# Layer 2's down projection in a seven-product form over six pairs of inner tiles, in a two-layer FNet + GLU kernel

## The chip, the cores and the metric

One core of one Trainium2 chip runs the whole program in one launch. The metric is device time in microseconds (us). TensorE (PE) multiplies, VectorE (DVE), ScalarE (ACT) and GpSimd (POOL) do the elementwise work, and transfers are started from SyncE's queue (SP) and from GpSimd's queue. PSUM has eight banks, each of 512 fp32 numbers in 128 partitions.

## The reference

`x` is 2048 tokens by 640. Two layers, each a Fourier mixing and a gated linear unit (GLU), both with a residual:

```python
def _A_ref(x, dft_seq_re, dft_seq_im, dft_hid_re, dft_hid_im):
    a = jnp.einsum("bsd,ed->bse", x, dft_hid_re)
    b = jnp.einsum("bsd,ed->bse", x, dft_hid_im)
    return jnp.einsum("ts,bse->bte", dft_seq_re, a) - jnp.einsum("ts,bse->bte", dft_seq_im, b)

def _B_ref(x, w_gate, w_up, w_down):          # 640 x 1728, 640 x 1728, 1728 x 640
    g = jnp.einsum("bsd,df->bsf", x, w_gate)
    u = jnp.einsum("bsd,df->bsf", x, w_up)
    return jnp.einsum("bsf,fd->bsd", _sigmoid(g) * u, w_down)

for _ in range(2):
    x = x + _A_ref(_layernorm(x), dft_seq_re, dft_seq_im, dft_hid_re, dft_hid_im)
    x = x + _B_ref(_layernorm(x), w_gate, w_up, w_down)
```

All is fp32. The same weights serve both layers.

## The kernel before

**Numbers.** A value is kept as two fp16 parts, HI and LO, and a product is three matmuls (`PASSES`: HI x HI, HI x LO, LO x HI) added up in PSUM. To make parts, ScalarE copies a value to fp16 (HI), and VectorE subtracts that copy from it (LO).

**Tiling.** The tokens are four blocks (`NB`) of 512, each four token tiles of 128. The inner size 1728 is 13 tiles of 128 (0 to 12) and a tail tile (13) of 64, which takes two passes. The output's 640 columns are two halves of 320 (`EH`). X (all tokens, fp32) stays on the chip. The rest lives in slots of one large buffer, `big`, which an allocator (`Slots`) gives out in units while the program is built.

**Order.** Nothing is scheduled by a planner: the order is written out by hand. `steps` is a list of steps, each with its matmuls (`mm`) and what follows them (`post`); `at(u, f, ...)` puts a job (a load, a split, a test) at a fractional time u in steps, and the jobs between two steps are issued there. An engine's instructions run in the order of issue, and so do the transfers of a queue.

**A layer's mixing** uses the symmetries of the Fourier matrices. As the matrices are inputs, the program reads them and tests these symmetries as it runs: GpSimd's queue loads pieces (L1293, L1310, L1353) into two rooms, VectorE compares them (L1299 to L1302), ScalarE squares and sums the differences (L1277). If a test fails, a general path runs in place of this one. For layer 2 the loads of these tests are spread evenly from 8 steps into block 0's gate-up to the end of block 2's.

**A layer's GLU**, block by block: gate and up for the block, then the down.
- Block 0's gate-up (`gate_up`, L1051): per inner tile 30 matmuls of 512 columns, each tile a step of its own; the tiles' PSUM banks come from a pool of eight, oldest first (`bank`, `free_bank`). Beside block 0 run the last combinations of the mixing for later tokens (`combine`, `join_hidden`, `add_hidden`, L920 to L940), in layer 2 partly beside block 1.
- Blocks 1 to 3 (`seven`, L1097): gate and up in a form with seven products. Two inner tiles share a step of 108 matmuls of 256 columns, in this order, with the counts of a step: `part_one` 12, `part_two` 18, `part_four` of an earlier tile 9, `part_six` 12 (the first that reads S), `part_four` 9, `part_five` 12, `part_seven` 18, `part_three` 18. Snaps (L1101) copy a PSUM chain to SBUF. `gate`, `up` and `up_parts` of the two tiles of the step before are issued between them: the sigmoid, the multiplications (L1153, L1155) after the sums (L1133, L1134), the parts of h (L1164, L1165). The last step has tile 12 and the tail (L1180, L1227 to L1231).
- Weights come back from DRAM for each block: `load_s` loads G (320 KB), S (512 KB, L1024) and U (192 KB) of one tile on SP's queue, about two steps ahead of the tile.
- The down (`down`, L1244): per token tile 41 products x 2 halves, 328 matmuls of 320 columns for a block; the evictions (L1259) add PSUM to X, and in layer 2 `store_x` stores the result right behind (L382 to L386 on SP's queue, and an indirect store, L378, on GpSimd's for two token tiles).

The down's loop before:

```python
order = [(j, hp, wp, e) for j in range(j0, j1) for hp, wps in (PASSES if j < NF else PASSES[:1])
         for wp in wps for e in es]
for j, hp, wp, e in order:
    nc.tensor.matmul(held["pd", e][0][:, :EH], held["ht", j].parts[hp][:, i * P : (i + 1) * P],
                     held["w", 2, j].parts[wp][:, e * EH : (e + 1) * EH], ...)
```

## Time and profile before

| | |
|---|---|
| median of 3 runs | 1162.23 us (1160.39 to 1162.62) |
| the profiled execution | 1158.61 us |
| its span | 1156.8 us |
| granted TensorE clock, mean | 0.999 |
| TensorE busy | 1127.3 us, 97%, 8784 matmuls |
| VectorE busy | 738.5 us, 64% |
| ScalarE busy | 507.7 us, 44% |
| GpSimd busy | 368.4 us, 32% |
| layer 2's GLU in the profile | 649.2 to 1150.4 us |

In a row of the chain the columns are the start, the length, the engine, what it is and its count. In a row of the windows: the stretch, its length, then busy time and count of PE, PEld (weight loads), DVE, ACT, POOL, then the granted clock, the DMA engines' busy share and GB/s. In a row of the groups: line, engine, operation, output<-input with shapes, count | busy us, mean ns of one | idle time of the engine just before them and what ended it. In a row of the timeline: start, length, engine, line, and in brackets the idle time before and its releaser.

### The profile page before, as it was taken

To read this page: it belongs to the slowest core of one execution; us is meant where nothing else is said; L and a number is where in the kernel's file an instruction comes from. 1 tells how busy PE (TensorE), PEld (TensorE's weight loads), DVE (VectorE), ACT (ScalarE), POOL (GpSimd) and SP (SyncE) were. 2 spreads that over 40 slices of the span, in tenths; PEclk is the share of its full clock that TensorE was granted. 3 is DMA by queue.
4 is the path that set the end of the run, shared out by engine and by line. 5 is a ranking of instruction groups with operands and counts; after the bars stand their busy time and mean duration, and the time that the engine had idled before them with its cause. 6 is when DMAs were issued, how large, how long until landed. Compare 5 with 4: busy or idle time off the path is not lost.

```text
span 1156.8 us, 22767 instructions
## 1 busy us (share of the span) xinstructions
PE 1127.3 (97%) x8784; PEld 860.0 (74%) x8784; DVE 738.5 (64%) x1636; ACT 507.7 (44%) x1094; POOL 368.4 (32%) x581
## 2 busy tenths in 40 slices
...
GB/s 267 148 46 236 241 355 281 259 209 212 144 265 182 252 179 194 264 191 258 47 18 110 190 200 73 129 264 262 222 142 258 247 270 56 199 240 184 132 19 38
DMA packets 158693, 216.46 MB, mean 187 GB/s; under 512 B 70194, under 2 KB 103883, under 8 KB 158574
## 3 DMA queue, kind: packets, MB, share of 16 engines
...
## 4 chain that ended last, share of the span: by engine, by line
PE 84%; DMA 2%; ACT 1%; POOL 1%; DVE 0%; issue 0%; SPq 0%; DVEq 0%; POOLq 0%
PE acc L1097 40%; PE acc L1244 31%; PE acc L1051 8%; PE acc L855 2%; PE acc L1180 2%; PE acc L773 1%; DMA kept_s<-big 1%; DMA kept_w<-big 1%; ACT big L236 1%; DVE big L238 0%; POOL big L1001 0%; PE acc L523 0%; ACT big L479 0%; ACT big L480 0%; POOL big L999 0%
## 5 line engine op out<-in xcount | busy, mean ns | idle before, releaser
L1097 PE MATMUL acc<-big 128*128 128x256 f16 x4212 | 462.8, 273 | 0.0
L1097 PEld LDWEIGHTS <-big 128*128 128x128 f16 x4212 | 412.1, 98 | 48.2
L1244 PE MATMUL acc<-big 128*128 128x320 f16 x2624 | 357.7, 299 | 0.0
L1244 PEld LDWEIGHTS <-big 128*128 128x128 f16 x2624 | 256.7, 98 | 99.7
L1293 POOL DMA_DIRECT2D big<-in_ct x256 | 175.1, 689 | 232.5 <-DVE big L1302 108.0
L1101 ACT ACTIVATE big<-acc 128x256 f32<-128x256 f32 x312 | 116.1, 381 | 208.9 <-PE acc L1097 207.5
L1051 PE MATMUL acc<-big 128*128 128x512 f16 (+1 forms) x990 | 176.5, 340 | 0.8 <-ACT big L236 0.5
L1051 PEld LDWEIGHTS <-big 128*128 128x128 f16 x990 | 96.5, 98 | 79.8 <-ACT big L236 1.0
L1277 ACT ACTIVATE big<-big 128x768 f32<-128x768 f32 (+8 forms) x104 | 79.4, 764 | 112.5 <-DVE big L1302 80.4
L1165 DVE TENSOR_TENSOR big<-big 128x512 f16<-128x512 f32 x78 | 53.8, 689 | 108.9 <-ACT big L1164 108.9
L1259 DVE SCALAR_TENSOR_TENSOR big<-acc,big 128x320 f32<-128x320 f32 x64 | 28.4, 484 | 91.6 <-PE acc L1244 91.5
L238 DVE SCALAR_TENSOR_TENSOR big<-big 128x640 f16<-128x640 f32 (+6 forms) x81 | 64.4, 833 | 2.9 <-ACT big L236 2.3
L1143 ACT ACTIVATE big<-big 128x512 f32<-128x512 f32 x78 | 47.9, 627 | 41.4 <-DVE big L1134 41.2
L236 ACT ACTIVATE big<-big 128x640 f16<-128x640 f32 (+7 forms) x81 | 50.7, 665 | 16.6 <-POOL big L1001 5.3
L1310 POOL DMA_DIRECT2D big<-in_ct x40 | 27.3, 686 | 94.9 <-ACT big L1277 47.3
L1134 DVE TENSOR_TENSOR big<-big,acc 128x512 f32<-128x512 f32 x78 | 53.1, 681 | 3.3 <-PE acc L1097 3.1
L1164 ACT ACTIVATE big<-big 128x512 f16<-128x512 f32 x78 | 48.8, 626 | 7.1 <-DVE big L1155 6.3
L1153 DVE SCALAR_TENSOR_TENSOR big<-acc,big 128x256 f32<-128x256 f32 x78 | 32.6, 418 | 27.9 <-PE acc L1097 22.4
L1299 DVE TENSOR_TENSOR big<-big 128x256 f32<-128x256 f32 x64 | 26.6, 416 | 36.8 <-DMA big<-in_ct 36.8
L855 PE MATMUL acc<-big 128*128 128x321 f16 (+3 forms) x324 | 48.8, 300 | 1.0 <-DVE big L238 1.0
L1300 DVE TENSOR_TENSOR big<-big 128x256 f32<-128x256 f32 x64 | 26.9, 421 | 30.9 <-DMA big<-in_ct 30.9
L509 ACT ACTIVATE big<-big 128x384 f16<-128x384 f32 (+2 forms) x48 | 28.9, 647 | 37.6 <-DVE big L491 17.9
...
## 6 DMA issues: line engine op xcount, KB each, us to landing
...
big<-in_ct POOLq DMA_DIRECT2D x256, 128.0 KB, 4.7
...
big<-in_ct POOLq DMA_DIRECT2D x32, 256.0 KB, 3.9
...
```

The costliest lines, as they stand in the source:

```text
L236: nc.scalar.activation(dh, src, AF.Copy, scale=s)
L238: nc.vector.scalar_tensor_tensor(dl, src, s, dh, op0=OP.mult, op1=OP.subtract)
L855: nc.tensor.matmul(ps[:m, :EC], z[:, at : at + m], w[:, 384 * wp : 384 * wp + EC], start=(d == 0 and zp == HI and wp == HI), stop=(d == ND ...
L1051: nc.tensor.matmul(ps, w[wp][:, d * P : (d + 1) * P], xt[:, xp, :], start=(d == 0 and wp == HI and xp == HI), stop=(d == ND - 1 and wp == LO))
L1097: nc.tensor.matmul(ps, wt, xt, start=start and n == 0, stop=n == len(todo) - 1, skip_group_check=not start)
L1101: nc.scalar.activation(dst, ps, AF.Copy)
L1134: nc.vector.tensor_tensor(v, v, other, op=OP.add)
L1164: nc.scalar.activation(s.parts[HI], v, AF.Copy)
L1165: nc.vector.tensor_tensor(s.parts[LO], v, s.parts[HI], op=OP.subtract)
L1244: nc.tensor.matmul(held["pd", e][0][:, :EH], held["ht", j].parts[hp][:, i * P : (i + 1) * P], held["w", 2, j].parts[wp][:, e * EH : (e + 1 ...
L1277: nc.scalar.activation(v, v, AF.Square, accum_out=new_sum()[:p])
L1293: nc.gpsimd.dma_start(v[:, g], bass.AP(ct.tensor, (r * S + row) * S, [[P, NS], [d * S, 16], [1, P]]))
```

## The change

In layer 2 the downs of all four blocks are written in a seven-product form. Inner tiles 0 to 11 make six pairs (`NP`). For a pair, h is a 2 x 2 matrix of parts (two halves of 256 tokens by two inner tiles) and the down weights another (two inner tiles by two halves of 320 columns). Seven products replace eight; four sums of h (A, AS) and four sums of weights (T1 to T4) are formed in exchange. The seven products go into four PSUM chains for each token tile (`CHAIN`), and a chain is added to X after every product (`READ`), which is 16 evictions for a block. Tiles 12 and 13 stay as they were (`REST`). The down's matmuls are 7 x 2 x 6 x 3 = 252 and 40, in place of 328.

With it go:
- `first_parts`, `second_parts`, `sum_parts` form and split the sums of h in the gate-up stages, in place of `gated_parts` and `up_parts`' two operations;
- T1 to T4 are formed from the raw weights in layer 1's downs of blocks 1 and 2 (`load_raw`, `make_t`, `split_t`, `keep_t`) and kept in DRAM. T1 comes with the down weights; T2, T3 and T4 (983 KB each) are loaded in each block of layer 2 on GpSimd's queue (`load_t`). `load_others` and `test_others` load and test the halves of weights that no longer come whole;
- stores of blocks 0 to 2 are issued in the next block's gate-up (`store_later`);
- layer 2's tests are spread anew: 11 in block 0's gate-up, 16 and 15 around blocks 1 and 2, and a test follows its load by 1.4 paces in place of one;
- all of layer 2's combines and joins lie in block 0's gate-up;
- for tiles from 4 on, `load_s` is split: S about one step ahead of its use, U at the step (before: all two steps ahead); for tiles 0 to 3 the loads move later in the down before;
- the allocator gets fixed places for A and AS and a limit for the others, G and U of a tile share one slot, and a row is written to DRAM and read again in layer 1;
- the scales `DS` and `PH` change by powers of two.

The core of the diff:

```diff
-DS = 2.0**11
+DS = 2.0**9
...
+NP = 6
+PAIRED = (), (0, 1, 2, 3)
...
+    def store_later(b, g, c):
+        if b < NB - 1:
+            at(block[b + 1] + 2.2 + 1.2 * g + c.start / D, store_x, b, g, c)
+        else:
+            store_x(b, g, c)
...
-    def load_s(j):
-        nc.sync.dma_start(take(5, "G", j).f16, kept["w", 0, j])
-        if ("S", j) not in held:
+    def load_s(j, do="GSU"):
+        if "G" in do:
+            v = take(8, "GU", j).f32
+            held["G", j], held["U", j] = Slot(v[:, : 5 * UNIT], None), Slot(v[:, 5 * UNIT :], None)
+            nc.sync.dma_start(held["G", j].f16, kept["w", 0, j])
+        if "S" in do and ("S", j) not in held:
             nc.sync.dma_start(take(8, "S", j).f16, kept["s", j])
-        nc.sync.dma_start(take(3, "U", j).f16.rearrange("p (q c) -> p q c", q=2),
-                          kept["w", 1, j].rearrange("p (q c) -> p q c", q=2)[:, :, 256:])
+        if "U" in do:
+            nc.sync.dma_start(held["U", j].f16.rearrange("p (q c) -> p q c", q=2),
+                              kept["w", 1, j].rearrange("p (q c) -> p q c", q=2)[:, :, 256:])
...
-    def gated_parts(j):
+    def gated_parts(j, paired=False):
+        if paired and j < 2 * NP:
+            if j % 2 == 0:
+                first_parts(j // 2, held["hf", j].f32)
+            else:
+                second_parts(j // 2, held["hf", j - 1].f32, held["hf", j].f32)
+                sum_parts(j // 2)
+                for i in (j - 1, j):
+                    drop("hf", i)
+            return
...
+    def up_parts(j, paired):
         if j not in late:
             return
         late.remove(j)
+        if paired and j < 2 * NP:
+            if j % 2 == 0:
+                first_parts(j // 2, held["hv", j].f32)
+            else:
+                second_parts(j // 2, held["hv", j - 1].f32, held["hv", j].f32)
+                for i in (j - 1, j):
+                    drop("hv", i)
+            return
...
+            if paired and j > 0:
+                sum_parts(j // 2 - 1)
...
+    def first_parts(p, v):
+        a = both(take(6, "A", p, top=UNITS - 8 * NP), 768)[:, :, :256]
+        f = take(8, "af", p).f32
+        nc.vector.tensor_tensor(f[:, 512:768], v[:, :256], v[:, 256:], op=OP.subtract)
+        nc.scalar.activation(a[:, 0], v[:, :256], AF.Copy)
+        nc.vector.tensor_tensor(a[:, 1], v[:, :256], a[:, 0], op=OP.subtract)
+    def second_parts(p, v, w):
+        a, f = both(held["A", p], 768)[:, :, 256:], held["af", p].f32
+        s1, s2, s4 = (f[:, 256 * n : 256 * (n + 1)] for n in (0, 1, 3))
+        nc.scalar.activation(a[:, 0], w, AF.Copy)
+        nc.vector.tensor_tensor(s1, v[:, 256:], w[:, 256:], op=OP.add)
+        nc.vector.tensor_tensor(s2, s1, v[:, :256], op=OP.subtract)
+        nc.vector.tensor_tensor(s4, w[:, :256], s2, op=OP.subtract)
+        nc.vector.tensor_tensor(a[:, 1], w, a[:, 0], op=OP.subtract)
+    def sum_parts(p):
+        f, s = held["af", p].f32, both(take(8, "AS", p, top=UNITS), 1024)
+        for c in (slice(0, 512), slice(512, 1024)):
+            nc.scalar.activation(s[:, 0, c], f[:, c], AF.Copy)
+        for c in (slice(0, 512), slice(512, 1024)):
+            nc.vector.tensor_tensor(s[:, 1, c], f[:, c], s[:, 0, c], op=OP.subtract)
+        drop("af", p)
...
+    def make_t(p):
+        v, w = (held["dr", 2 * p + k].f32 for k in range(2))
+        b11, b12, b21, b22 = v[:, :EH], v[:, EH:], w[:, :EH], w[:, EH:]
+        nc.vector.tensor_tensor(b11, b12, b11, op=OP.subtract)
+        nc.vector.tensor_tensor(b12, b22, b12, op=OP.subtract)
+        nc.vector.tensor_tensor(b22, b22, b11, op=OP.subtract)
+        nc.vector.tensor_tensor(b21, b21, b22, op=OP.subtract)
...
+    def load_t(n, b, p=None):
+        if n == 1:
+            nc.sync.dma_start(take_t(n, b, p), kept["t", n][:, p])
+            return
+        take_t(n, b, 0)
+        v = held["T4"].f16 if n == 4 else t_place(n, b)
+        nc.gpsimd.dma_start(v.rearrange("p (k q c) -> p k q c", k=NP, q=2), kept["t", n])
...
+    LEFT = {1: ("A", 0), 2: ("A", 1), 4: ("A", 2), 5: ("AS", 0), 6: ("AS", 1), 7: ("AS", 2), 3: ("AS", 3)}
+    RIGHT = {1: (0, 0), 2: (1, 0), 3: (1, 1)}
+    CHAIN = {1: "a", 2: "c", 5: "b", 3: "b", 4: "d", 6: "a", 7: "a", 8: "a"}
+    READ = {1: (0, 0), 2: (0, 0), 5: (1, 1), 3: (0, 1), 4: (1, 0), 6: (0, 1), 7: (1, 0), 8: (1, 1)}
+    REST = (2, 3, 4, 8)
...
+            for n, i in todo:
+                first = (CHAIN[n], i) not in held
+                if first:
+                    held[CHAIN[n], i] = bank()
+                mms = []
+                for p in range(NP) if n < 8 else ():
+                    a = both(held[LEFT[n][0], p], 256, LEFT[n][1])[:, :, i * P : (i + 1) * P]
+                    if n in RIGHT:
+                        r, e = RIGHT[n]
+                        w = both(held["w", 2, 2 * p + r], EH, e)
+                    else:
+                        w = take_t(n if n == 4 else n - 4, b, p)
+                    mms += [(a[:, ap], w[:, wp]) for ap, wps in PASSES for wp in wps]
+                r, e = READ[n]
+                c = (i + 2 * r) * P
+                for j in range(2 * NP, NF + 1) if n in REST else ():
+                    mms += [(held["ht", j].parts[hp][:, c : c + P], held["w", 2, j].parts[wp][:, e * EH : (e + 1) * EH])
+                            for hp, wps in (PASSES if j < NF else PASSES[:1]) for wp in wps]
+                for m, (a, w) in enumerate(mms):
+                    nc.tensor.matmul(held[CHAIN[n], i][0][:, :EH], a, w, start=first and m == 0, stop=m == len(mms) - 1,
+                                     skip_group_check=not first)
...
+                ps, k = held[CHAIN[n], i]
+                r, e = READ[n]
+                g = i + 2 * r
+                xe = X[:, b * TB + g, e * EH : (e + 1) * EH]
+                nc.vector.scalar_tensor_tensor(xe, ps[:, :EH], CB, xe, op0=OP.mult, op1=OP.add)
+                if n in REST:
+                    del held[CHAIN[n], i]
+                    free_bank(k)
...
+            if b in PAIRED[layer]:
+                if first or b < last:
+                    order = [[(n, 0), (n, 1)] for n in (1, 5, 2, 3, 6, 4, 7, 8)]
+                else:
+                    order = [[(m, i), (n, i)] for i in range(2) for m, n in ((1, 2), (6, 5), (7, 3), (4, 8))]
+                steps += [down_pairs(b, todo, not first) for todo in order]
+                for n, u in ((2, d0 + 0.3), (3, d0 + 0.6), (4, d0 + 2.6)):
+                    at(u if first or b < last or n == 4 else block[b] + 2 + n, load_t, n, b)
+                continue
...
-                at(block[0] + 1.6 + 0.8 * n if q == 1 else (block[0] + 14.6 if q == 2 else block[1] + 3.5) + n, f, q, *a)
+                at(block[0] + 1.6 + 0.8 * n if q == 1 else (block[0] + 14.6 + n, block[1] + 3.5 + n)[q - 2] if first else block[0] + 4 * q - 4 + 0.7 * n, f, q, *a)
...
+                    elif q[0] == 0 and j > 3 and b in PAIRED[layer]:
+                        k = j % 2
+                        for what, v in (("G", u - 2 - 0.5 * k), ("S", u - (0.5 if j == NF - 1 else 1 + 0.5 * k)), ("U", u - k)):
+                            at(v, load_s, j, what)
                     elif q[0] == 0:
-                        at(u - 2 - 0.5 * (j % 2) if j > 3 else block[b] - ((4, 3, 2, 1.5) if first and b == 1 else (8, 7.9, 4.5, 3.5))[j], load_s, j)
+                        at(u - 2 - 0.5 * (j % 2) if j > 3 else block[b] - ((4, 3, 1, 0.5) if b - 1 in PAIRED[layer] else (4, 3, 2, 1.5) if first and b == 1 else (8, 7.9, 4.5, 3.5))[j], load_s, j)
...
+                u = block[2 + p // 3] - 5.5 + 1.5 * (p % 3)
+                for k in range(2):
+                    at(u - 1.5, load_raw, 2 * p + k)
+                at(u, make_t, p)
+                for k in range(2):
+                    at(u + 0.5 + 0.5 * k, split_t, 2 * p + k, (0,))
+                    at(u + 0.9 + 0.5 * k, split_t, 2 * p + k, (1,))
+                    at(u + 1.4 + 0.5 * k, keep_t, 2 * p + k)
...
-            u0, u1 = block[0] + 8, block[2] + 14
+            free = (block[0] + 4, block[0] + 13.5, 11), (block[1] - 7, block[1] + 12.5, 16), (block[2] - 7, block[2] + 12.5, 15)
...
+            at(v + (0 if first else 0.4 * (w - v)), test, *key)
+            at(v + (0.7 if first else 0.8) * (w - v), square_rest)
```

180 lines of the change are left out of this document (149 added, 31 removed).

## The prediction

> **What bounds the kernel now.** I read the page first, then the chain of waits, the windows of layer 2, the groups by form, and single stretches of the timeline.
>
> ```profile
> span 1156.8 us, 22767 instructions
> PE 1127.3 (97%) x8784; PEld 860.0 (74%) x8784; DVE 738.5 (64%) x1636; ACT 507.7 (44%) x1094; POOL 368.4 (32%) x581
> ```
> TensorE (PE) is busy 97% of the span, the next engine, VectorE (DVE), 64%. A share of busy time is a mean, so the chain has to show that no other engine ends a stage.
>
> ```profile
> 774.94 71.39 PE acc L1097 x654
> ...
> 855.50 44.55 PE acc L1244 x328
> ...
> 1025.17 71.39 PE acc L1097 x654
> ...
> 1105.82 44.57 PE acc L1244 x328
> 1150.39 0.02 issue
> 1150.41 0.49 DVE big L1259
> ```
> Each piece starts where the one ahead ends: in layer 2 the matmuls stand back to back, and the end is the last matmul plus one eviction and a store. So a matmul taken out of a down (L1244) comes off the time in full, unless it uncovers a wait. The cover is in the windows by stage (columns: PE, PEld, DVE, ACT, POOL busy, clock, DMA share, GB/s):
>
> ```profile
> 649.20:730.40 81.20, 81.20 (x437) 42.65 (x437) 53.20 (x103) 20.01 (x39) 22.94 (x42) 1.00 0.41 127
> ...
> 774.90:855.50 80.60, 80.60 (x741) 72.22 (x739) 63.21 (x149) 43.89 (x101) 39.88 (x67) 1.00 0.68 211
> 855.50:900.05 44.55, 44.55 (x330) 32.12 (x329) 24.61 (x58) 13.44 (x26) 20.48 (x29) 1.00 0.91 248
> 900.05:980.60 80.55, 80.55 (x741) 72.17 (x739) 49.05 (x122) 42.41 (x99) 21.68 (x40) 1.00 0.57 187
> ...
> 1025.20:1105.80 80.60, 80.60 (x740) 72.14 (x739) 37.95 (x77) 38.98 (x101) 8.09 (x7) 1.00 0.57 165
> ```
> VectorE's room in the gate-up stages is 28 us in block 0, 17 in block 1, 31 in block 2, 43 in block 3. The clock is full, so a stretch without a wait scales with its matmuls.
>
> **What goes.** A block's down falls from 328 matmuls of 320 columns to 292 (seven products x 2 token tiles x 6 pairs x 3 passes = 252, and 40 for tiles 12 and 13). A matmul is 44.55/328 = 0.1358 us, so a block gives 36 x 0.1358 = 4.89 us, and four blocks 19.56 us. No matmul is added elsewhere.
>
> **What VectorE and ScalarE get.**
>
> ```profile
> L1165 DVE TENSOR_TENSOR big<-big 128x512 f16<-128x512 f32 x78 | 53.8, 689 | 108.9 <-ACT big L1164 108.9
> L1164 ACT ACTIVATE big<-big 128x512 f16<-128x512 f32 x78 | 48.8, 626 | 7.1 <-DVE big L1155 6.3
> L1133 DVE TENSOR_TENSOR big<-big 128x256 f32<-128x256 f32 x78 | 32.6, 417 | 9.9 <-ACT big L1101 9.8
> L1101 ACT ACTIVATE big<-acc 128x256 f32<-128x256 f32 x312 | 116.1, 381 | 208.9 <-PE acc L1097 207.5
> L1259 DVE SCALAR_TENSOR_TENSOR big<-acc,big 128x320 f32<-128x320 f32 x64 | 28.4, 484 | 91.6 <-PE acc L1244 91.5
> ```
> Per pair VectorE gains five operations of 256 elements (four sums, and one low half that is split off) and one of 512: 5 x 0.42 + 0.69 = 2.8 us, 16.7 us per block. ScalarE gains one copy of 256 and one of 512, 1.0 us per pair, 6 us per block; it has over 36 us of room, so that costs nothing by itself. A down has 16 evictions where it had 8: 8 x 0.484 = 3.9 us, beside 20 us of room. But VectorE's operations follow one another more closely than they last:
>
> ```profile
> 735.26 0.42 DVE L500 TENSOR_TENSOR big<-big 128x256 f32<-128x256 f32 x1
> 735.59 0.41 DVE L501 TENSOR_TENSOR big<-big 128x256 f32<-128x256 f32 x1
> 735.93 1.28 DVE L510 TENSOR_TENSOR big<-big 128x384 f16<-128x384 f32 x2
> ```
> Starts lie 0.33 us apart where the records last 0.42. I count what queues by such gaps, about 0.075 us under the duration, and keep full durations as the bad end.
>
> **Block 0.** All of layer 2's combines and joins, 11 tests and the pairs' parts now share its gate-up. In the order of the built programs tiles 3 to 9 hold 55 us of VectorE work by gaps (64 by durations) against 29 before, in 7 x 30 matmuls of 512 columns, 45.5 us by L1097's rate for 256. VectorE is then some 9.5 us behind. The gate-up's PSUM banks carry three tiles (19.5 us) before TensorE must wait, so nothing is lost there; at the down the third product in a bank needs its first eviction done 16 us in, and VectorE gets there at about 15.2, with two waits for GpSimd's part of a join and some for loads ahead of it. I take 1.5 us, between 0 and 4.
>
> **Blocks 1 and 2: when S comes.** Tiles 4 to 12 now load S about one step ahead of its use instead of two. For an odd tile the room comes free only when the earlier pair's last low half is split off: matmul 90 of a step of 108 (9.8 us of 11.8), a snap 0.38, a copy 0.63, a subtraction 0.69, so 11.5 us. The next step uses S at its matmul 46, at 16.8. That leaves 5.3 us. What such a load (512 KB) takes over the run:
>
> ```profile
> L1024 SPq DMA_DIRECT2D big<-kept_s x75: 319/383/2047, 222.7 to 1083.3; - x75
> DMA to landing us min/median/max: 4.0/5.5/14.8
> ```
> and in its worst stretch, 304 to 348 us, in layer 1:
> ```profile
> DMA to landing us min/median/max: 4.0/9.4/14.8
> ```
> So the median alone is 0.2 us late. Behind a waiting load on SP's queue stand the U load of the same tile and the next tile's G. In block 1 four tiles (5, 7, 9, 11) are in this place, and VectorE, with 63.2 us before and some 16 added less what moved out, adds 1.5 to 2 us of lag in the middle steps: 3.5 us lost, from 0.5 (landing at 4.0 and no lag) to 9. Its down has the same third product; VectorE reaches the eviction at 12.8 us of 16, so 0 (to 3). In block 2 with 49.05 us only one tile lies so close: 1 us, 0 to 4.
>
> **Block 3.** Here the order of products is another: (2,0), which includes tile 12, comes second, so tile 12's high half is needed after 36 matmuls, 4.89 us into the down, and its low half 0.3 later.
>
> ```profile
> 1104.83 0.69 DVE L1165 TENSOR_TENSOR big<-big 128x512 f16<-128x512 f32 x1 [1.91 <-ACT big L1164]
> ...
> 1109.98 0.69 DVE L1134 TENSOR_TENSOR big<-big,acc 128x512 f32<-128x512 f32 x1
> 1111.37 0.42 DVE L1153 SCALAR_TENSOR_TENSOR big<-acc,big 128x256 f32<-128x256 f32 x1 [0.69 <-ACT big L1143]
> ...
> 1112.88 0.69 DVE L1165 TENSOR_TENSOR big<-big 128x512 f16<-128x512 f32 x1 [0.76 <-ACT big L1164]
> ```
> The high half is done at 1112.83, 7.0 us into the down, the low half at 7.75. Two copies and two subtractions of the last pair's sums come ahead of that chain, so 7.7 and 8.4. TensorE stands for 2.8 us, and 0.5 more for the low half: 3.3 us, at least 2.6, at most 6 if all four come ahead. Two S loads there add 0.2. This gap is the one place where a clock could fall:
>
> ```profile
> 26.48 2.47 PE L350 MATMUL twin<-big 128*128 128x320 f32 x4 [2.69 <-DMA big<-in_x]
> 36.10 2.50 PE L350 MATMUL twin<-big 128*128 128x320 f32 x4 [7.15 <-ACT big L356]
> ```
> After 7.15 us of idling the same four matmuls take as long as after 2.69, so I add nothing. The Trainium skill ("TensorE: Matmul & The Clock Gate", section "HAM oscillation — how this bites in real kernels") holds that an idle gap above some 3.4 us puts the array at half clock for about 1.67 us; by it, as an estimate, the sum would be 0.8 us longer. These rows don't agree with it.
>
> **The end, and edits at nothing.** The last evictions and stores are two of each, as before, but one store now stands close behind an indirect one (L378):
>
> ```profile
> DMA to landing us min/median/max: 6.5/7.0/7.5
> ```
> It is issued some 3 us ahead of the end, so 0.3 us, up to 3.4 if that landing counts. For what is moved into layer 1 and onto GpSimd's queue these rows serve:
>
> ```profile
> L238 DVE SCALAR_TENSOR_TENSOR big<-big 128x640 f16<-128x640 f32 x41 | 38.5, 957 | 2.9 <-ACT big L236 2.3 <-POOL big L1001 0.6
> L657 DVE TENSOR_TENSOR big<-big 128x320 f32<-128x320 f32 x16 | 7.0, 482 | 0.0
> big<-in_ct POOLq DMA_DIRECT2D x32, 256.0 KB, 3.9
> ```
> T1 to T4 cost layer 1's downs 4 x 0.48 + 2 x 0.96 = 3.8 us of VectorE per pair, three pairs in a down; evictions there hold two of eight banks, so a down of 44.6 us hides them. T2, T4 and T3 (983 KB each) are asked for on GpSimd's queue at the start, by 16 us and near the start of a down, and first used 22.3, 27.2 and 33.4 us into it. In proportion to 256 KB in 3.9 us such a load takes 15 us, which would make T4 3.8 us late in each block; at the 248 GB/s that the down of block 1 moved it takes 4. I take the latter, so nothing. Stores moved to the next block leave SP's queue in the down and join it where it has loads only every 2 to 3 us: nothing. The first two G loads of a block are now issued late in the down, where such a store or a T load could make them up to 3 us late; I take nothing.
>
> **The sum.** -19.56 + 1.5 + 3.5 + 1.0 + 3.5 + 0.3 = -9.8 us. The profiled run took 1158.61 us (span 1156.8 and 1.8 around it), so it becomes 1148.8. The median of the runs, 1162.23, lies 3.6 above it: **1152.5 us**, its own range 1146 to 1161 (all losses near their small or their large ends).
>
> **Rivals.**
> - *S comes late everywhere (slower).* Seven loads (four in block 1, one in block 2, two in block 3) have a lead of 5.3 us. At 9.4 us, the median of the crowded stretch, each stalls TensorE for 4.1 us, with some of VectorE's lag 4.4: 31 us, and 6.3 of other losses, less 19.6: +17.8, **1180 us**. For it: 12 new T loads of 983 KB and the later issue crowd the same rings (DMA share 0.91 in a down). Against: layer 2's loads in the gate-up stages are not in that stretch. It decides from a landing of 5.3 + (19.6 - 6.3)/7 = 7.2 us on. 0.17.
> - *VectorE sets the pace.* If operations cost their full durations, block 0's lag doubles to 20 us and uncovers about 9.5, block 1 about 8, block 2 two and block 3 3.5: 23 less 19.6 is +3.4, **1165.6 us**. For it: 64 us of work in 45.5. Against: starts 0.33 us apart. The Trainium skill ("VectorE: DVE Perf Modes", section "The DRAIN you can't avoid") says that the next operation does not start until the pipe is empty; the rows from 735.26 on, which start ahead of the former's end, do not agree. 0.08.
> - *The covers hold.* Only block 3's wait stays: -19.6 + 3.5 = -16.1, **1146 us**. For it: landings of 4.0, and VectorE's gaps. 0.15.
>
> **How the numbers follow.** The forecast has 0.60. Within 0.2% (2.3 us, about what a measurement of this kernel can tell from no change) lie 1159.9 to 1164.5: 0.05 of the forecast's high end, and half of VectorE's rival. Faster: 0.55 + 0.15 = 0.70; same 0.05 + 0.04 = 0.09; slower 0.04 + 0.17 = 0.21. The range takes in the whole gain with 2 us below it and VectorE's rival with 2 above, 1144 to 1168, and leaves out the late loads.
>
> **What would show it.** TensorE has 8640 matmuls. Downs: 39.7 us in block 2, 43 in block 3 with an idle row of about 3 us ahead of the matmuls that read tile 12; a wait for a DMA ahead of the first S products of block 1's later steps; VectorE over 70 us in block 0's gate-up with TensorE unbroken. It is wrong if block 1 has waits over 2 us at each step, if gate-up of block 0 stretches beyond 83 us, or if an opening or layer 1 stage changes by more than 1 us.

## The result and the profile after

| | before | after |
|---|---|---|
| median | 1161.80 us (1160.39 to 1162.62) | 1229.12 us (1219.65 to 1239.41) |
| ratio, 95% interval | | 1.0554 (1.0462 to 1.0645) |
| the profiled execution | 1158.61 us | 1219.65 us |
| its span | 1156.8 us | 1217.8 us |
| granted TensorE clock, mean | 0.999 | 0.977 |

The changed kernel is slower by 5.5%; 1152.5 us had been forecast. One of its four runs (1239.41 us) was in a slower state and is left out of the ratio, though not of the median. Its trace is of its fastest execution. First the page of after: the head line, the busy times, the clock in 40 slices, and the chain by engine.

```profile
span 1217.8 us, 22936 instructions
PE 1127.4 (93%) x8640; PEld 850.9 (70%) x8640; DVE 829.6 (68%) x1849; ACT 533.1 (44%) x1154; POOL 379.1 (31%) x594
PEclk9999999999999999799999999999999999988999
PE 48%; DVE 16%; DMA 15%; issue 4%; ACT 3%; POOL 2%; SPq 1%; DVEq 0%; ACTq 0%; POOLq 0%
```

The 144 matmuls are gone (8640), and yet TensorE is busy as long as before (1127.4 against 1127.3 us), where 19.56 us less were due: matmuls have become slower somewhere. In the chain of waits TensorE carries 48% where it carried 84%; VectorE and transfers carry 31% where they carried 2%. Where that lies is seen by stages. From the timeline of TensorE, each stage's length (before, after, and the loss against what the stage would take without a wait, which for a down of layer 2 is 39.7 us):

| stage | before | after | lost |
|---|---|---|---|
| layer 1, gate-up of block 1 | 80.6 | 80.6 | 0 |
| layer 1, gate-up of block 2 | 80.6 | 88.1 | 7.5 |
| layer 1, gate-up of block 3 | 80.6 | 100.7 | 20.1 |
| layer 2, gate-up of block 0 | 81.1 | 81.1 | 0 |
| layer 2, down of block 0 | 44.5 | 46.8 | 7.1 |
| layer 2, gate-up of block 1 | 80.6 | 89.6 | 9.0 |
| layer 2, down of block 1 | 44.5 | 39.8 | 0.1 |
| layer 2, gate-up of block 2 | 80.5 | 84.3 | 3.8 |
| layer 2, down of block 2 | 44.5 | 43.1 | 3.4 |
| layer 2, gate-up of block 3 | 80.7 | 103.5 | 22.8 |
| layer 2, down of block 3 | 44.7 | 45.9 | 6.2 |
| end, after the last matmul | 6.5 | 7.1 | 0.6 |

The losses add up to 80.6 us, the gain is 19.56, and the span grew by 61.0. The windows of layer 2 in after (columns as before):

```profile
757.90:804.60 46.70, 41.83 (x293) 29.07 (x292) 35.53 (x82) 16.95 (x33) 28.86 (x51) 0.96 0.83 200
804.60:894.30 89.70, 83.02 (x741) 72.76 (x740) 68.77 (x166) 45.00 (x107) 36.22 (x60) 0.98 0.76 238
894.30:934.00 39.70, 39.70 (x294) 28.53 (x292) 28.01 (x64) 14.32 (x27) 15.40 (x24) 1.00 0.86 220
...
1061.30:1164.80 103.50, 88.63 (x738) 75.10 (x739) 52.64 (x113) 42.92 (x111) 13.03 (x12) 0.92 0.66 196
1164.80:1210.70 45.90, 41.87 (x294) 28.85 (x292) 15.23 (x42) 4.01 (x8) 3.58 (x5) 0.96 0.13 45
```

The third row is the form at its best: no wait, full clock, 39.70 us for a down. In the others TensorE's busy time is itself too long (88.63 us for what took 80.60), at a clock below 1. The timeline of TensorE in after names the waits (idle time before, and who ended it, in brackets):

```profile
383.56 43.72 PE L1169 MATMUL acc<-big 128*128 128x256 f16 x384 [4.37 <-ACT big L1173]
...
501.26 28.87 PE L1169 MATMUL acc<-big 128*128 128x256 f16 x240 [15.24 <-ACT big L1173]
...
761.10 14.04 PE L1445 MATMUL acc<-big 128*128 128x320 f16 x101 [0.72 <-DVE big L1333]
779.30 25.53 PE L1445 MATMUL acc<-big 128*128 128x320 f16 x174 [4.15 <-DVE big L1462]
...
810.13 2.23 PE L1169 MATMUL acc<-big 128*128 128x256 f16 x10 [4.65 <-DMA big<-kept_w]
...
894.26 39.91 PE L1445 MATMUL acc<-big 128*128 128x320 f16 x292
...
936.95 8.24 PE L1169 MATMUL acc<-big 128*128 128x256 f16 x74 [2.13 <-DMA big<-kept_w]
...
1068.71 28.14 PE L1169 MATMUL acc<-big 128*128 128x256 f16 x237 [6.55 <-DMA big<-kept_w]
1099.11 8.72 PE L1169 MATMUL acc<-big 128*128 128x256 f16 x63 [2.25 <-DMA big<-kept_s]
...
1154.00 2.50 PE L1261 MATMUL acc<-big 128*128 128x256 f16 x15 [3.59 <-DMA big<-kept_w]
...
1172.14 13.01 PE L1445 MATMUL acc<-big 128*128 128x320 f16 x82 [2.24 <-ACT big L1245]
1186.93 23.80 PE L1445 MATMUL acc<-big 128*128 128x320 f16 x174 [1.78 <-DMA big<-kept_t]
```

There are four sorts: snaps of ScalarE in layer 1 (L1173), evictions by VectorE in block 0's down (L1462), the first weights of a block (kept_w), and in block 3 weights all along. Each has its experiments below.

**The clock.** The row at 501.26 has 240 matmuls in 28.87 us; at 71.39/654 us each they take 26.2. Windows of after, around the gaps that end at 383.56 and at 501.26:

```profile
383.60:388.00 4.40, 4.40 (x26) 3.24 (x26) 3.79 (x11) 4.32 (x11) 3.35 (x6) 0.62 0.27 103
388.00:392.00 4.00, 4.00 (x39) 3.59 (x38) 3.66 (x9) 1.04 (x3) 1.79 (x5) 1.00 0.61 197
...
501.30:505.00 3.70, 3.70 (x18) 2.56 (x18) 2.39 (x7) 1.14 (x4) 2.27 (x4) 0.50 0.86 256
505.00:509.00 4.00, 4.00 (x32) 3.27 (x30) 3.48 (x9) 1.95 (x6) 1.47 (x2) 0.82 0.95 281
509.00:515.00 6.00, 6.00 (x57) 5.39 (x55) 4.27 (x12) 1.48 (x4) 1.13 (x2) 1.00 1.04 368
```

After a gap the granted clock is 0.50 to 0.62 for some 4 us, and for longer after the 15 us gap. Adding up, piece by piece, what the matmuls after such gaps took over the full rate gives 16.7 us in after: one fifth of the losses, and part of the stages' losses above.

### The profile page after: what moved, and what is told of

It reads as the page before. It is cut to its first block, busy times and chain, and to the rows that moved or that the text cites. A ratio compares the mean times of both kernels' runs of the same rounds, so it can differ in the third digit from the quotient of the medians.

```text
span 1217.8 us, 22936 instructions
## 1 busy us (share of the span) xinstructions
PE 1127.4 (93%) x8640; PEld 850.9 (70%) x8640; DVE 829.6 (68%) x1849; ACT 533.1 (44%) x1154; POOL 379.1 (31%) x594
## 4 chain that ended last, share of the span: by engine, by line
PE 48%; DVE 16%; DMA 15%; issue 4%; ACT 3%; POOL 2%; SPq 1%; DVEq 0%; ACTq 0%; POOLq 0%
PE acc L1169 26%; PE acc L1495 11%; DMA big<-kept_w 6%; PE acc L1445 5%; DMA big<-in_ct 3%; PE acc L891 2%; DMA big<-big 2%; PE acc L1261 1%; DMA big<-kept_s 1%; DMA kept_t<-big 1%; PE acc L1114 1%; PE acc L809 1%; DVE wmax L247 1%; DVE big L536 1%; DMA kept_s<-big 1%
## 5 line engine op out<-in xcount | busy, mean ns | idle before, releaser
L1169 PE MATMUL acc<-big 128*128 128x256 f16 x4212 | 477.8, 277 | 44.9 <-ACT big L1173 21.7
L1169 PEld LDWEIGHTS <-big 128*128 128x128 f16 x4212 | 416.9, 99 | 103.7 <-issue 30.2
L1173 ACT ACTIVATE big<-acc 128x256 f32<-128x256 f32 x312 | 113.8, 380 | 193.4 <-PE acc L1169 192.2
L1495 PE MATMUL acc<-big 128*128 128x320 f16 x1312 | 178.9, 299 | 0.0
L1445 PE MATMUL acc<-big 128*128 128x320 f16 x1168 | 163.9, 303 | 10.9 <-DVE big L1462 6.1
L1495 PEld LDWEIGHTS <-big 128*128 128x128 f16 x1312 | 128.4, 98 | 49.8
L1445 PEld LDWEIGHTS <-big 128*128 128x128 f16 x1168 | 115.1, 99 | 58.9 <-issue 8.5
L1114 PEld LDWEIGHTS <-big 128*128 128x128 f16 x990 | 96.4, 98 | 79.9 <-ACT big L254 1.1
L254 ACT ACTIVATE big<-big 128x640 f16<-128x640 f32 (+7 forms) x93 | 59.5, 675 | 74.9 <-DMA kept_t<-big 44.5
L256 DVE SCALAR_TENSOR_TENSOR big<-big 128x640 f16<-128x640 f32 (+6 forms) x93 | 73.9, 830 | 13.9 <-ACT big L254 13.2
L1215 ACT ACTIVATE big<-big 128x512 f32<-128x512 f32 x78 | 48.1, 627 | 51.2 <-DVE big L1206 50.6
L1246 DVE TENSOR_TENSOR big<-big 128x512 f16<-128x512 f32 x42 | 28.9, 688 | 47.3 <-ACT big L1245 47.3
L1462 DVE SCALAR_TENSOR_TENSOR big<-acc,big 128x320 f32<-128x320 f32 x64 | 29.5, 487 | 36.4 <-PE acc L1445 36.4
L1551 DVE TENSOR_TENSOR big<-big 128x256 f32<-128x256 f32 x64 | 26.9, 421 | 25.7 <-DMA big<-in_ct 25.7
```

The costliest lines, as they stand in the source:

```text
L254: nc.scalar.activation(dh, src, AF.Copy, scale=s)
L256: nc.vector.scalar_tensor_tensor(dl, src, s, dh, op0=OP.mult, op1=OP.subtract)
L1114: nc.tensor.matmul(ps, w[wp][:, d * P : (d + 1) * P], xt[:, xp, :], start=(d == 0 and wp == HI and xp == HI), stop=(d == ND - 1 and wp == LO))
L1169: nc.tensor.matmul(ps, wt, xt, start=start and n == 0, stop=n == len(todo) - 1, skip_group_check=not start)
L1173: nc.scalar.activation(dst, ps, AF.Copy)
L1215: nc.scalar.activation(v, v, AF.Sigmoid, scale=SG)
```

## The experiments

In each, one part of the change is put elsewhere or left out. A ratio is always to the kernel before, measured again beside the run. The stages are told as above; a wait before a stage's first matmul counts to the stage ahead of it. "Form alone" is 1161.8 - 19.56 = 1142.2 us.

**e1: T1 to T4 made in layer 1's gate-ups of blocks 1 and 2, not in its downs.** In after, ScalarE's splits of the T values wait for SyncE's queue. Three views: the waits of after, ScalarE's timeline, SyncE's timeline in the down ahead of the 15.24 us gap.

```profile
ACT big L254 <- DMA kept_t<-big: 44.5, 6, 25.7
```
```profile
490.40 0.74 ACT L254 ACTIVATE big<-big 128x640 f16<-128x640 f32 x1 [25.71 <-DMA kept_t<-big]
```
```profile
446.00 34.59 SPq L542 DMA_TRANSPOSE big<-big  x4
480.68 1.00 SPq L1355 DMA_DIRECT2D big<-in_wd  x2
481.78 0.38 SPq L1061 DMA_DIRECT2D big<-kept_w  x1
482.26 0.38 SPq L1063 DMA_DIRECT2D big<-kept_s  x1
482.69 0.55 SPq L1065 DMA_DIRECT2D big<-kept_w  x1
483.29 1.10 SPq L1377 DMA_DIRECT2D kept_t<-big  x2
```

A split needs one of two buffers; a buffer is free once `keep_t` (L1377) has stored it; that store stands on SyncE's queue behind four transposes, the queue's entry for which is 34.59 us long. ScalarE stands for 25.7 us at L254, the snaps queue behind it, and TensorE waits for the snaps.

```diff
-                u = block[2 + p // 3] - 5.5 + 1.5 * (p % 3)
+                u = block[1 + p // 3] + 9.1 + 1.6 * (p % 3)
-            fixed(XU + (j < NP) * XTU + 20 + 5 * (j % 2), 5, "tp", j)
+            fixed(XU + (j >= NP) * XTU + 20 + 5 * (j % 2), 5, "tp", j)
```


> Only the place of the making of T1 to T4 in layer 1 is changed: it moves from the downs of blocks 1 and 2 into the gate-up stages of blocks 1 and 2 (9.1 to 14.2 steps in), same operations, same transfers. Theory A: layer 1's 28 us (7.5 in block 2's gate-up, 20.2 in block 3's) come from the order of SyncE's queue: the writes of T stand behind four transposes and the next block's loads, two buffers make ScalarE wait for them, and all that ScalarE feeds waits. Then both gate-up stages return to 80.6 us, the downs to 44.6, layer 1 gives back 26 to 28 us, and the run takes about 1192 us (profiled about 1191). Rival B: it is the amount of work (VectorE, ScalarE, transfers) that layer 1 can't hide: then blocks 1 and 2's gate-up grow by 10 us each in its place, and the time stays above 1210. Layer 2's stages do not change by either: 46.7, 89.7, 39.7, 84.3, 43.0, 103.5, 45.9 within 3 us each.

Measured: 1204.61 us, 1.0371 (1.034 to 1.0402) where after had 1.0554: some 21 us less, with an uncertainty of about half of that, as after's runs lie far apart. Layer 1's gate-ups of blocks 1 to 3 take 84.1, 83.3 and 80.6 us: 6.2 us lost in place of 27.6, with the same operations and transfers. That the place of the T values' making cost layer 1 most of this time is shown; that it did so through the stores behind the transposes is read from the three views.

**e2: G and U of a block's first two tiles asked for ahead of the second pair of transposes** (on top of e1). In after the first weights of a block wait behind the mixing's transposes of the block before; SyncE's timeline of after, and the same place in e2:

```profile
775.09 25.21 SPq L542 DMA_TRANSPOSE big<-big  x4
800.40 0.53 SPq L1061 DMA_DIRECT2D big<-kept_w  x1
```
```profile
755.74 8.92 SPq L542 DMA_TRANSPOSE big<-big  x2
764.71 0.58 SPq L1061 DMA_DIRECT2D big<-kept_w  x1
765.33 0.58 SPq L1065 DMA_DIRECT2D big<-kept_w  x1
767.54 11.79 SPq L542 DMA_TRANSPOSE big<-big  x2
```
```diff
+                    elif q[0] == 0 and j < 2 and b - 1 in PAIRED[layer]:
+                        at(block[b] - (7.2, 4.5)[j], load_s, j, "GU")
+                        at(block[b] - (4, 3)[j], load_s, j, "S")
```


> As the run with T made later, and in layer 2 the loads of G and U of a block's first two tiles are issued ahead of the second pair's transposes (7.2 and 4.5 steps ahead of the block, in place of 4 and 3); their S loads stay. Theory C: the gaps of 4.65, 2.1 and 6.55 us at matmul 6 of blocks 1, 2 and 3, and the throttled clock behind the long ones (about 2 us each), come from G standing behind the transposes in SyncE's queue. Then these gaps go, blocks 1 and 3 gain 6 to 8 us each, block 2 two: 13 to 18 us less than the run with T later. Rival D: the ring's bandwidth in the down is the limit, whatever the order: then the same time is lost in other loads of the same stretch (S of tile 0 or 1), and the run differs by under 4 us.

Measured: 1188.69 us, 1.0236 (1.0205 to 1.0267), 15.9 us less than e1. Gate-ups of blocks 1 to 3: 82.9, 82.7, 91.5 us (e1: 89.2, 84.6, 104.4); the waits for G at the three openings are gone. Block 2's down grew from 45.4 to 48.7 us. In after the load is asked for at 800.4 and the block begins at 804.7.

**e3: S and U half a step to one step earlier** (on top of e1), the forecast's "S comes late".

```diff
-("S", u - (0.5 if j == NF - 1 else 1 + 0.5 * k))
+("S", u - 1.5 - 0.5 * k)
```


> As the run with T made later, and in layer 2's paired blocks S of tiles from 4 on is issued half a step earlier (1.5 and 2 steps ahead of use in place of 1 and 1.5; tile 12 as the others). Theory E (S late by the room that the last subtraction frees): the order in the queue doesn't matter, S still waits for its room, and holds the queue longer for the G and U behind it: same or slower by up to 10 us. Theory F (S is issued late): the small gaps in front of S (0.6 to 2.3 us, six of them) go: 4 to 8 us faster.

Measured: 1199.38 us (1192.90 to 1206.12), 1.0304 (1.0261 to 1.0347); its interval and e1's overlap. Block 1's gate-up is longer (93.2 against 89.2), block 3's shorter (95.4 against 104.4). No clear gain: asking for S half a step earlier does not remove the waits.

**e4: layer 2's 42 spread tests left out** (on top of e1).

```diff
             u, v, w = spots[q : q + 3]
+            if not first:
+                continue
```


> As the run with T made later, with the 42 run-time tests of the sequence matrices left out in layer 2 (their loads, comparisons and squares; the result is not tested for layer 2's matrices). Theory G: the tests' 128 KB loads and VectorE's in-order waits for them make block 0's eviction late (4.15 us and the throttle behind it) and delay the transposes, so the downs and the starts of blocks 1 and 2 lose 15 us to them: block 0's down 40 to 41 us, block 1's gate-up 82 to 85, block 2's down 40; block 3 (no such tests in it, but in block 2's down none either from two steps before its end) stays within 5 us of 103. In all 15 to 22 us less than the run with T later. Rival D (order in SyncE's queue alone): under 6 us.

Measured: 1187.66 us, 1.0242 (1.0200 to 1.0283). TensorE's timeline of e4 in blocks 0 and 1:

```profile
737.32 39.89 PE L1445 MATMUL acc<-big 128*128 128x320 f16 x292
777.05 71.56 PE L1169 MATMUL acc<-big 128*128 128x256 f16 x654
...
857.61 39.89 PE L1445 MATMUL acc<-big 128*128 128x320 f16 x292
897.34 71.56 PE L1169 MATMUL acc<-big 128*128 128x256 f16 x654
```

Without these tests blocks 0 to 2 have no wait up to block 2's down: all that was lost there needs them. At the openings it needs G's place behind the transposes too, since e2 removed those waits with the tests in place. Block 3 stays as it was (104.0 us).

**e11 and e12: of the tests, the loads alone, and the work alone** (on top of e1). e12 has no loads of the spread tests; VectorE compares what lies there. e11 has the loads, without VectorE's comparisons.

```diff
# e12
-            at(u, load, *key)
+            if first:
+                at(u, load, *key)
# e11
         a, b, c, d = (v[:, 2 * P * g : 2 * P * (g + 1)] for g in range(4))
+        if plain[0]:
+            return rest.append(v[:, 2 * P :])
```


> The counterpart: the loads of layer 2's 42 tests are left out, VectorE's comparisons and ScalarE's squares (scaled to zero) stay and work on what lies in the rooms; the general path is never taken. If VectorE's work is the cause: block 0's down 44 to 49 us, gate-ups of blocks 1 and 2 84 to 89. If transfers and the waits for them are: 39.7 to 41 and 80.6 to 82. By both theories block 2's down and block 3's gate-up stay long (45 and 104), since the hidden tests are in their old place.

> As the run with T made later (1204.6), with VectorE's comparisons of layer 2's 42 tests left out; their loads and ScalarE's squares stay, so the rooms are freed as before or sooner, and the flag is set so that the general path is never taken. It parts what the run without tests took away together. If VectorE's work and its in-order waits for the loads are the cause: block 0's down 39.7 to 41, gate-ups of blocks 1 and 2 81 to 83, as without tests. If the tests' transfers are it (they slow transposes and G, S and U): block 0's down 44 to 49, gate-ups 85 to 90, as with them.

e12: 1192.97 us, 1.0262 (1.0208 to 1.0317); its interval and e4's overlap. Its block 0's down is 46.6 us as in after, the gate-ups of blocks 1 and 2 are 81.1 and 81.5:

```profile
761.01 25.51 PE L1445 MATMUL acc<-big 128*128 128x320 f16 x174 [4.04 <-DVE big L1462]
786.36 62.06 PE L1169 MATMUL acc<-big 128*128 128x256 f16 x567
```

So block 0's down waits for VectorE's work (4.04 us of the 4.15 in after). The waits of blocks 1 and 2 need the tests' loads: as traffic, or as loads that VectorE waits for in order. e12 takes both away and does not tell them apart. e11 went the other way, 1219.40 us, 1.0478 (1.0436 to 1.0519). Its block 0's down has no wait for VectorE, which agrees with e12. But from the start of a down to the next block's first matmul it takes 60.4 us in block 0 and 56.0 in block 1, of which 13.72 and 9.31 us are waits for G. Ahead of the first of these, four transposes kept SyncE's queue for 42.90 us (24.47 in e1). Its loads ran only a little ahead of e1's (51 of 148 issued by 750 us, against 42), so why the transposes took longer is not shown.

**e5: layer 2's last tests (of the hidden-side matrices, `in_wh`) written later** (on top of e1).

```diff
-(r, k), 15.5 + 1.7 * (4 * r + k), 2.8)
+(r, k), 22.3 + 0.95 * (4 * r + k), 1.6)
```


> As the run with T made later, and the tests of the hidden matrices (14 loads with short rows) move from block 2's down into block 3's gate-up. Theory H: in block 2's down these loads slow the first pair's transposes (18 to 22 us in place of 8), the second pair's VectorE work waits in order for the room that these free, so an eviction and the loads of block 3's first tiles are late; then block 2's down falls from 45.4 to 40-42 us, the 6 to 7 us gap at matmul 6 of block 3's gate-up goes, and the run is 10 to 15 us faster than 1204.6. Rival I (T4's 983 KB load and the S, U and G loads behind it slow the transposes): both stages stay within 3 us.

Measured: 1204.34 us, 1.0333 (1.028 to 1.0385), as e1. A miss: of the 16 row loads four were still issued in block 2's down (1024.2 to 1028.0 us; eight in e1), over 30 us ahead of the block that they were written into, and the other twelve fell into block 3's gate-up. The down took 48.2 us (45.4 in e1), the gate-up 94.5 (104.4).

**e13: e4 without these last tests as well.**

```diff
-            for load, test, key, u, later in tests:
+            for load, test, key, u, later in ():
```


> As the run with T made later, with layer 2's 42 tests and the 14 tests of the hidden matrices left out; no order is changed. Theory K: block 3's loss is the hidden tests: their loads slow the transposes of block 2's down, and VectorE waits for them in order. Then block 2's down takes 39.7 us, block 3's gate-up 81 to 86 (3.6 of it the tail's weights behind S of tile 12 in SyncE's queue), its down 42 to 44 (tile 12 and T4): 1148 to 1156 us. Theory L (the form's own transfers: S just in time, T2 and T3 in block 3's gate-up, stores): the gate-up stays above 92.

Measured: 1153.95 us (1150.01 to 1165.47), 0.994 (0.9906 to 0.9974): 33.7 us less than e4. Block 2's down and block 3's gate-up fell from 47.3 and 104.0 to 39.7 and 84.8 us. How the transfers differ is in the views of the DMA issues from block 2's down into block 3's gate-up (count, KB, median us to landing), of after:

```profile
big<-kept_s SPq DMA_DIRECT2D x8, 512.0 KB, 15.5
big<-in_wh POOLq DMA_DIRECT2D x16, 200.0 KB, 10.0
```
of e13:
```profile
big<-kept_s SPq DMA_DIRECT2D x8, 512.0 KB, 5.7
```
and of the kernel before, from the start of block 2's down (980 to 1072 us):
```profile
big<-kept_s SPq DMA_DIRECT2D x12, 512.0 KB, 7.9
big<-in_wh POOLq DMA_DIRECT2D x16, 200.0 KB, 7.3
```

So the test loads alone do not make S late: in before the same 16 stood beside S, which landed in 7.9 us. It takes them together with what the change adds. The transposes of block 2's down keep SyncE's queue for 26.17 us in after, 30.04 in e4 and 18.72 in e13.

The chain of waits of after in block 2's down and block 3 names what came late, the mixing's transposes and two weight loads:

```profile
1028.40 18.44 DMA big<-big x2
...
1056.38 12.29 DMA big<-kept_w
...
1094.78 16.12 DMA big<-kept_w
```

e1, e4 and e13 split the loss by taking things away in turn. By their ratios (after 5.54% above the kernel before, e1 3.71, e4 2.42, e13 0.60 below it) that is some 21 us for T, 15 for the spread tests and 35 for the last tests, and 13 us stay above the form alone. In another order the shares could be others, as e2 shows for the openings.

**e6, e7, e8, e9: orders and tests together.** e6 has e2's and e5's edits, T's raw loads half a step earlier, and the order of products of blocks 0 to 2 in the last down too. e7 has e6's edits with the spread tests kept to the gate-ups and the last tests from 8 steps into block 3 on; e8 is e6 without the spread tests. e9 is e8 with the last tests of e7 and a last down by other pairs of products.

```diff
# e6
-                if first or b < last:
+                if True:
# e7
+            free = (block[0] + 4, block[0] + 12, 5), (block[1], block[1] + 13, 14), (block[2], block[2] + 13, 14), (block[3], block[3] + 7, 9)
+            (r, k), 30 + 0.65 * (4 * r + k), 1.1)
# e9
+                    order = [[(1, 0), (5, 0)], [(6, 0), (2, 0)], [(3, 0), (7, 0)], [(1, 1), (5, 1)], ...]
```


> Together: T made in the gate-up stages of layer 1 with its raw loads half a step earlier, G and U of the first two tiles ahead of the second transposes, the hidden tests in block 3's gate-up, and the last block's products in the order of the other blocks. The 42 tests stay where the change put them. By the theory that the layer 1 part (7 us left, from VectorE's wait for raw weights), the queue's order and the hidden tests are causes of their own: layer 1 within 3 us of before, block 1 to 3's gate-up 82 to 86, block 2's down 40 to 42, block 3's down 41; block 0's down still 46 to 50, since nothing is taken from VectorE there: 1150 to 1170 us. Rival J (VectorE's lag from block 0 and the tests set all of them): block 1 to 3 lose what e1 showed, above 1180.

> As the run before in this set, and the 42 tests are placed in the gate-up stages alone: 5 in block 0, 14, 14 and 9 in blocks 1 to 3, and the hidden tests behind them in block 3; nothing is left out. If the tests' VectorE work in block 0 and their transfers in the downs are what makes evictions and transposes late, block 0's down comes to 40 to 42 us, the starts of blocks 1 to 3 have no gap over 1 us, and the gate-up stages pay 0 to 4 us each for 27 us of VectorE work: 1142 to 1158 us. If VectorE in the gate-up stages has no room for it (69 us busy in block 1 before the move), S comes late there and blocks 1 and 2 take 88 to 92 us each: 1165 to 1180.

> As the run with all the orders together, with layer 2's 42 tests of the sequence matrices left out. This is the form's worth with the cover back: if all losses of the changed kernel are the three causes (T's queue, the tests, block 3's transposes), downs take 39.7 us in all four blocks, gate-ups 80.6 to 82, and the run comes to the before's time less 19.56 plus 1 to 6 us: 1143 to 1149 us. If the form itself costs something that no order removes (S behind the last subtraction, two more evictions in a bank), it stays above 1155.

> As the run with all orders together and the 42 tests of layer 2 left out, with two further changes of order: the hidden tests stand 8 steps into block 3's gate-up behind block 2's indirect stores in GpSimd's queue (in that run GpSimd reached their loads at 991 us, during block 2's down, though they had been written later), and the last block's products go 1, 5, 6, 2, 3, 7 for the first token tile, with product 4 after the second tile's 1 and 5, so that the last store is not an indirect one. Theory H again (these short-row loads make the transposes take 18 to 25 us): block 2's down 39.7 to 41 us, block 3's gate-up 81 to 86, the end after the last matmul 6 to 7 us: 1139 to 1147 us. Rival (T4 and the next block's loads slow the transposes): block 2's down stays near 50 and block 3's gate-up near 94: 1165 to 1172.

| | us | ratio | down 0, gate-up 1, down 1, gate-up 2, down 2, gate-up 3, down 3 |
|---|---|---|---|
| e6 | 1198.99 | 1.0311 (1.0276 to 1.0346) | 50.3, 84.8, 40.0, 82.5, 51.8, 95.1, 39.9 |
| e7 | 1177.03 | 1.0131 (1.0088 to 1.0174) | 39.7, 88.6, 39.7, 89.2, 39.7, 91.8, 39.9 |
| e8 | 1176.57 | 1.0133 (1.0088 to 1.0177) | 39.7, 80.6, 39.7, 80.6, 50.4, 94.2, 39.9 |
| e9 | 1170.68 | 1.0084 (1.0048 to 1.012) | 39.7, 80.6, 39.7, 80.6, 39.7, 93.4, 48.1 |

e6, e8 and e9 missed the times expected of them by 24 to 29 us; e7 came out as its second branch said. The order of blocks 0 to 2 takes the last down to 39.9 us, but the end grows to 10.6 us in e6. With no test in a down (e7) all downs are free of waits, and the cost is paid in the gate-ups (88.6, 89.2). e9 against e8: with the last tests out of block 2's down it gets back its 10.7 us, but the last down, whose order is also another, takes 8.2 more, and there VectorE is late:

```profile
1123.66 37.78 PE L1445 MATMUL acc<-big 128*128 128x320 f16 x256 [5.31 <-DVE big L1462]
```

**e14: all of layer 2's tests left out, orders mended** (T as in e6, G as in e2, e9's last down, the tail's weights half a step earlier, layer 1's tests spread as in e15 below).

> As the run before in this set, with the orders mended: G and U of the first two tiles ahead of the second transposes, the tail's weights ahead of S of tile 12, the last block's products in the later order, T's raw weights earlier, and layer 1's tests thinned to three in each stretch where T is made, the rest up to block 3's down. Theory K: all gate-ups 80.6 to 81.5 and all downs 39.7 to 40.5 in layer 2, layer 1 within 3 us: 1140 to 1146 us, the before's less 17 to 20. If S just in time costs something by itself, block 3's gate-up stays 2 to 4 us above.

Measured: 1145.69 us (1144.37 to 1148.74), 0.9862 (0.9818 to 0.9906): 16.6 of the form's 19.56 us (by the two traces 12.8, as the traced execution of before is 3.6 us under the median). Layer 1 has 81.4, 80.6 and 80.6 us, block 3 82.5 and 41.8. So the form is worth most of what its count of matmuls says, once layer 2's tests are away. The kernel before was not run without them, but in its layer 2's GLU TensorE has no gap that such a run could close.

**e10, e15, e16, e17, e18: whole kernels, with every test.** All have e14's T, G and last down (the tail's weights half a step earlier only from e15 on). But for e17, layer 2's spread tests lie in the gate-ups and the last steps of the downs (5 in block 0, then by turns 4, 9, 4, 9, 3, 8). Layer 1's keep out of the stretches where T is made (the later part of the gate-ups of blocks 1 and 2) in e10; in e15, e17 and e18 three stand in each of these, and the rest run 7 steps further; in e16 they stay as in after. The last tests come from 8 steps into block 3 on; e15 and e16 load them by 1280-byte rows. e17 puts eight of them into block 1, e18 all of them into the last down, with rooms of their own:

```diff
# e15
-            nc.gpsimd.dma_start(v[:, g], bass.AP(wh.tensor, (r * D + row) * D, [[P, ND], [d * D, 80], [1, P]]))
+            nc.gpsimd.dma_start(v[:, g], bass.AP(wh.tensor, (r * D + row) * D, [[EH, 2], [d * D, 64], [1, EH]]))
# e17
+            (r, k), -21.7 + 1.6 * (4 * r + k), 2.6)
# e18
+                at(d0 + 0.1 + 0.01 * n, load_hidden_rows, n // 4, n % 4)
+                at(d0 + (3 if n < 4 else 5) + 0.2 * (n % 4), test_hidden_rows, n // 4, n % 4)
```


> A version that leaves nothing out: as the run with the tests in the gate-up stages, with 11 of the 42 tests moved into the last three steps of the downs, the last block's products in the order of the run before, and layer 1's tests kept out of the stretches where T is made. If VectorE's load in the gate-up stages is what the 8 to 11 us per block there come from, each of blocks 1 to 3 gives back 3 to 6 us, the end 3.5, layer 1 three to five: 1150 to 1162 us. If transfers in the downs are as dear as work in the gate-up, downs of blocks 0 to 2 grow by as much: 1165 to 1178.

> Nothing left out: the 42 tests as in the earlier rearranged version, the hidden rows loaded in rows of 1280 bytes (ten tests of 64 rows in place of eight of 80) in the second half of block 3's gate-up, the hidden columns and the final test in its down, all orders mended, layer 1's tests thinned where T is made. By theory K block 3's gate-up comes to 83 to 87 and its down to 40 to 42; with layer 1 within 3 us: 1146 to 1156 us. If the tests' transfers in the down and gate-up stages still hold up G, S and U: 1160 to 1170.

> As the run before in this set, with layer 1's tests spread evenly as the change has them. Layer 1 then keeps the 6 to 7 us that it lost in the runs with T later: 4 to 7 us slower than the run before; layer 2's stages the same within 2 us. If thinning in one stretch makes the others too dense, as in the first rearranged version (21 us lost in layer 1), this one is faster by 3 to 12 us.

> Nothing left out: as the rearranged version with thinned tests in layer 1, with the eight hidden row tests in block 1's gate-up alone (1.6 steps apart, tested 2.6 steps, about 15 us, after their load), their rows loaded as the change has them, the hidden columns early in block 3's gate-up on GpSimd's queue, and the 42 tests in what is left: 8 in block 0, 11 in block 2's gate-up, 7 in block 3's, 13 in the ends of the downs, 3 at the start of the last down; the final test before the first indirect store. By theory K (VectorE waits in order for loads that land later than their test's turn) no stage of layer 2 is more than 2 us over 80.6 and 39.7 except block 3's, 3 to 5 over: 1145 to 1153 us, faster than before by 0.8 to 1.5%. If the tests' transfers are simply too many beside the form's, the stages that took them over lose what block 3 gains: 1158 to 1168.

> Nothing left out: as e15 (its 1163.6 us), with all 14 hidden tests in the last down: their loads start with the down into rooms of their own (six slots that are free there, the two rooms of the tests, and the place of block 3's x for the columns), VectorE's part comes 16 to 30 us later, the final test at 30 us; the last eight of the 42 tests are spread over all of block 3's gate-up, and T4 is loaded at the down's start. By theory K block 3's gate-up comes from 94.4 to 81-84 us, its down from 46.6 to 40-43, the rest as in e15: 1142 to 1152 us, faster than before by 0.9 to 1.7%. If block 3's loss is not VectorE's in-order waits for the hidden loads but S, U and G with T2, T3 and the stores, the gate-up stays above 88: 1156 to 1164. If the loads slow T4 or the end, the down takes 45 to 50.

| | us | ratio | layer 1's gate-ups 1 to 3; layer 2's stages as above |
|---|---|---|---|
| e10 | 1183.81 | 1.0172 (1.0117 to 1.0227) | 80.6, 89.6, 92.8; 39.7, 81.4, 40.1, 81.4, 39.7, 90.5, 46.6 |
| e15 | 1163.58 | 1.0026 (0.9998 to 1.0055) | 81.8, 80.7, 80.6; 39.7, 81.3, 40.1, 81.0, 39.7, 94.4, 46.6 |
| e16 | 1166.76 | 1.0044 (1.0025 to 1.0063) | 83.0, 83.5, 85.0; 39.7, 81.6, 39.8, 80.9, 39.7, 93.9, 48.0 |
| e18 | 1161.77 | 1.0012 (1.0000 to 1.0025) | 81.4, 80.6, 80.6; 39.7, 81.1, 40.2, 81.1, 39.7, 84.2, 47.3 |

(The traced execution of e16 took 1174.78 us, 8 above its median.) Layer 2's blocks 0 to 2 are nearly free of waits in all four, with the tests in them. e10 loses 21 us in layer 1, where its tests are crowded into less room; e15 spreads them wider and loses 1.3. e18 shows that block 3's gate-up falls from 94.4 to 84.2 us when the last tests leave it (its last eight spread tests lie wider there too); but its last down stays at 47.3 and its end is 10.6 us. e10, e15 and e18 came out above the times first expected of them. The chain of e18 there, and TensorE's timeline:

```profile
1106.88 14.42 DMA big<-in_wh
...
1131.48 4.95 DMA out<-big,rows
...
1142.57 0.81 DVE big L1462 x2
```
```profile
1143.41 1.49 PE L1445 MATMUL acc<-big 128*128 128x320 f16 x5 [3.64 <-DVE big L1462]
```

The evictions stand on VectorE's queue behind the last comparisons and the final verdict on them; ahead of that verdict VectorE stood for 6.03 us, up to 1141.08, for GpSimd's part of it. e17's time, 4278.93 us, is of another path, and not comparable: the general path's matmuls run from 1215.11 us on, behind layer 2. In the order of its program a load into a room (14.933 steps into block 3) stands just ahead of the squares of what lay there (14.937), so that test's sum was wrong; that this made the verdict fail follows from the program and was not tested apart. Up to there its downs took 41.8, 52.4, 51.0 and 46.5 us. No whole kernel is faster than the one before; e18 equals it.

## Why the prediction was wrong

The saving was right. What failed is the list of losses: the prediction put them at 9.8 us, and the trace of after has 80.6. Two steps that it put at nothing or nearly so make up most of it: the making of T in layer 1 (27.6 us) and block 3's gate-up (22.8). The other losses are 7.1 us in block 0's down, 12.8 in the gate-ups of blocks 1 and 2, 3.5 in their downs, 6.2 in block 3's down and 0.6 at the end. No rival went as far as the measured time either.

**Right.** A down without a wait takes 39.7 us for its 292 matmuls (894.26), so 4.89 us for a block; 8640 matmuls; VectorE's gaps (74.2 us of its work in block 0's gate-up, with TensorE unbroken at 81.1 us); ScalarE's room; the end, +0.6 for 0.3; tile 12's wait in block 3's down, 2.24 us at 1172.14 for 2.8 (that down lost 6.2 in all: 1.78 more at 1186.93 for a T load, which had been put at nothing, and clock). The sentence of the Trainium skill that the prediction quotes against VectorE's rival ("VectorE: DVE Perf Modes", section "The DRAIN you can't avoid") is followed there by one that lets an operation that isn't held start earlier, so the Trainium skill and the rows need not differ.

**"T1 to T4 cost layer 1's downs 3.8 us of VectorE per pair ... so a down of 44.6 us hides them": wrong, 27.6 us.** The step counted VectorE's work and forgot the splits' stores. These stand on SyncE's queue behind transposes, and ScalarE waits in order for them; made elsewhere, the same T values cost 6.2 us (e1). It was the prediction's own sign of error ("a layer 1 stage changes by more than 1 us").

**Block 0, "I take 1.5 us, between 0 and 4": 7.1 us.** The mechanism is the one forecast, VectorE behind at the third product; it arrives 21 us in, not 15.2. e12 shows that the tests' work does it without their transfers. 4.15 and 0.72 us are gaps, 1.7 is clock. (By the rate named, 7 x 30 matmuls of 512 columns are 45.8 us, not 45.5; nothing hangs on it.)

**"The first two G loads ... up to 3 us late; I take nothing": 4.65, 2.13 and 6.55 us of gap** at the openings of blocks 1 to 3, behind the four transposes; e2, which moves those G and U loads alone, gave back 15.9 us. The prediction looked at stores and T loads in front of G and not at the transposes, which the diff did not name but past which G had been moved.

**"Two S loads there add 0.2": 22.8 us in block 3's gate-up** (the 6.55 us above and the clock behind it included). The last tests were not costed at all, as their lines look the same in the diff. Nor does the section on the kernel before name them: in its trace they are loaded from 983.6 us, early in block 2's down, to 1100.3, with no wait of TensorE. In after they meet later G and S loads, T loads and longer transposes; S lands in 15.5 us, where it took 7.9 beside the same loads in before and 5.7 without them in e13, and block 3's gate-up is 19.2 us shorter without them (e13 against e4). Whether the 16 loads' bandwidth or VectorE's in-order wait for them weighs more there was not told apart.

**S in blocks 1 and 2 (3.5 and 1.0 us).** The gate-ups lost 9.0 and 3.8, but mostly at the opening. The forecast's place, an S load ahead of each odd tile, shows three gaps of 0.59 to 0.75 us there, asking earlier did not help (e3), and without the spread tests there is none (e4). The rival "S comes late everywhere" had the sign right, but by luck: the loss lies elsewhere, and where S was late, in block 3, it was so for another cause.

**The clock: "I add nothing": 16.7 us, within the losses above.** The prediction read two rows of the opening, four long fp32 matmuls after 7.15 us of idling, as a rule for the whole kernel. Those rows stand, at a clock of 1.00, but they do not hold for the fp16 stages, where after such a gap the clock is about half. The Trainium skill ("TensorE: Matmul & The Clock Gate", section "HAM oscillation — how this bites in real kernels") had it: a gap above some 3.4 us throttles. Here 34 of 35 such gaps in the fp16 stages of all traces did. The Trainium skill's price was low: from its 1.67 us at half clock comes an estimate of 0.8 us for a gap, and the common loss here is 1.7.
